# Batch 0 of a beacon-attention and maxout-FFN kernel: a new order of turns, score groups, quad loads and weight requests

## The chip, the cores and the metric

The kernel runs on one core of a Trainium2 chip. A core has five engines that work side by side: TensorE (PE in the profile; its weight loads are listed apart as PEld), VectorE (DVE), ScalarE (ACT), GpSimd (POOL) and SyncE (SP), which here only issues DMAs. Each engine runs its own instructions in order, and semaphores tie the engines together. The metric is the device time of one execution in microseconds; the median of several runs counts.

## What is computed

Attention with a causal mask, in which every query also sees 16 beacon keys without a mask, and behind it a feed-forward layer that takes the elementwise maximum of three projections. There are 8 batches of 8 heads, 576 tokens and a head size of 64; the model size is 512 and the inner size 768.

```python
scores = scale * np.matmul(q, k_all.transpose(0, 1, 3, 2))   # k_all, v_all: 16 beacons, then 576 tokens
scores = np.where(causal, -1000000000.0, scores)             # beacons are never masked
a = np.exp(scores - scores.max(-1, keepdims=True))
a /= a.sum(-1, keepdims=True) + 1e-09
attn = np.matmul(a, v_all)                                   # then x = attn as (tokens, 512)
h = np.maximum(np.maximum(x @ w1, x @ w2), x @ w3)
out = h @ w_out
```

## The kernel before

**Tiling.** Two heads make a pair (`p`, 4 pairs a batch, 32 in all), two pairs make a quad. Q and K of a pair are needed with the head dimension on partitions ("turned"). They are held in `qkT`, a ring of 4 pairs: first 576 columns of Q, then 16 beacon columns and 576 columns of K. For batches 0 to 3 PE turns them by transposes into PSUM, and DVE or ACT copies them out; for the later batches a DMA does it through DRAM.

**Steps of attention.** For a pair the scores are computed as K by Q in four groups (`emit_scores(p, gi)`): PE writes a two-bank tile `sc` of PSUM (two such tiles exist), and ACT takes the exponential of it into `at_sb` (line 469). `emit_masks` zeroes the causal part, on DVE with a table `tri` (L486) or on POOL with an affine select (L488). When both pairs of a quad are ready, `emit_pv(quad, hf)` multiplies by ones (for the sums) and by V, for one half `hf` of the queries (L532), into the two `pv` banks or, where it is asked for (`apart`), into two `fps` banks. `invert_sums` takes 1/sum as exp(-ln) on ACT (L552, L554), and `multiply` writes the result into `xT` on DVE (L564).

**FFN.** `emit_ffn` takes the next unit of a list: first units of the first matmul with weights 1 and 2 for half token blocks (L611), then units of the third weight (L592), then units of the second matmul (L628). Each unit is followed by a copy or a maximum on DVE. A unit is allowed once its part of `xT` is written.

**Order.** All runs under a schedule that is written out by hand. `start()` loads and turns the first pairs; then the list `first_steps` takes the 16 score groups of batch 0, each followed by the functions written beside it: `T` turns a half of a pair, `M` masks, `P` is attention times V, `V` casts a piece of the first V tile on POOL, `F` is an FFN unit, `CW` and `TW` cast and turn a quad of batch 1. From batch 1 on a loop takes two score groups, masks, PV and FFN units in turn, and calls what `plan` holds for the step. `next_load` takes the next load from a list; loads of q, k and v go through SP's DMA queue into a ring of 8 tiles `st`. The weights and the four-head quads of batch 0 are cast on the way and are requested by POOL (L309, L228). A gate is a one-column memset of the `st` tile by an engine: the DMA has to wait for it, and so can't start before that engine has come to that place of its queue.

**PSUM.** Two tiles `sc` of two banks, two `pv` banks, two `fps` banks. `keep_busy` issues matmuls on constants whose result nobody reads; it takes a bank for itself.

Of the kernel before, what the change touches and what calls it, by code (L numbers as in the profile page):

```python
# [16 lines left out]
def kernel(  # L17
# [13 lines left out]
    nc = tc.nc  # L31

    B, H, S, D = q.shape
    Nb = beacon_k.shape[2]
    NK = S + Nb
    scale = 1.0 / float(D) ** 0.5
    d_model, d_ff = moe_w1.shape
# [26 lines left out]
    n_quad = 2  # L64
    PPB = H // 2
# [4 lines left out]
    B_PE = 4  # L70
# [36 lines left out]
    def head(g, j):  # L107
        return 4 * g + j
# [29 lines left out]
    bT = const.tile([128, PPB, NB_PE], BF16, name="bT")  # L138
    bk32_0 = const.tile([Nb, H, D], FP32, name="bk32_0")
    bk16_0 = const.tile([Nb, H, D], BF16, name="bk16_0")  # L140
    bk32_1 = const.tile([NB_PE - Nb, H, D], FP32, name="bk32_1")
    bk16_1 = const.tile([NB_PE - Nb, H, D], BF16, name="bk16_1")
# [3 lines left out]
    busy = const.tile([128, 320], BF16, name="busy")  # L146
    nc.vector.memset(busy, 1.0)
    ident = const.tile([128, 128], BF16, name="ident")
# [4 lines left out]
    NT = 4  # L153
    qk_all = const.tile([128, NT, S + NKP], BF16, name="qkT")
    qkTs = [qk_all[:, i] for i in range(NT)]
    qTs = [z[:, 0:S] for z in qkTs]
    kTs = [z[:, S : S + NKP] for z in qkTs]
# [6 lines left out]
    def pv_bank(i, shape, dtype):  # L164
        return pv_psum.tile(shape, dtype, name=f"pv{i}")

    by_dve = nc.vector.tensor_copy
    by_act = nc.scalar.copy
    by_pool = nc.gpsimd.tensor_copy
# [8 lines left out]
    def new_stage(key):  # L178
        stage[key] = st_pool.tile([128, STW], FP32, name="st")
        return stage[key]  # L180

    def load_wide(quad, i, gate=None):
        b, g = divmod(quad, n_quad)
        st = new_stage(("wide", quad, i))

        if gate:
            gate.memset(st[:, 0:1], 0.0)
        src = (q, k)[i][b, head(g, 0) : head(g, 0) + 4]
        nc.sync.dma_start(
            out=st[:, 0 : 2 * WR * D].rearrange("p (x c) -> p x c", x=2),  # L190
            in_=src.rearrange("(x y) (p r) d -> (y p) x (r d)", y=2, r=WR),
        )
# [125 lines left out]
    def load_beacons(b0, b1, dst, queue=None):  # L318
        for b in range(b0, b1):
            (queue or nc.sync).dma_start(  # L320
                out=dst[Nb * (b - b0) : Nb * (b - b0 + 1)],
                in_=beacon_k[b].rearrange("h n d -> n h d"),
            )
# [60 lines left out]
        if r1 == WR:  # L384
            stage.pop(("wide16", quad, i))

    def turn_half(p, h, pv, q_copy=None):
        for i in range(2):
            src = stage.pop(("half16", p, h, i))
            if pv:  # L390
                bank = pv_bank(i, [128, 1024], BF16)
            else:
                bank = ffn_psum.tile([128, 1024], BF16, name="fps")
            ps = bank[:, 0:HALF]
            for r in range(HR):
                for e in range(2):
                    nc.tensor.transpose(
                        ps[64 * e : 64 * e + 64, r * QP : (r + 1) * QP],
                        src[:, e, r],
                        ident[0:QP, 0:QP],  # L400
                        tile_position=(0, 64 * e),
                    )
            x0 = i * Nb + HALF * h
            dst = (qTs, kTs)[i][p % NT][:, x0 : x0 + HALF]
            (q_copy if i == 0 and q_copy else by_dve)(
                dst.rearrange("d (p r) -> d p r", r=HR), ps.rearrange("d (r p) -> d p r", r=HR)
            )

    def place_beacons(p, copy):
        b, pi = divmod(p, PPB)  # L410
        copy(kTs[p % NT][:, 0:Nb], bT[:, pi, Nb * b : Nb * (b + 1)])

    def turn_quad(quad, i):
        for n, copy in enumerate((by_dve, by_act)):
# [10 lines left out]
    def keep_busy(n, cols=320, ffn=False):  # L425
        ps = ffn_psum.tile([128, 512], FP32, name="fps") if ffn else pv_bank(1, [128, 512], FP32)
        for _ in range(n):
            nc.tensor.matmul(
                ps[:, 0:cols], busy[:, 0:128], busy[:, 0:cols], start=True, stop=True
            )  # L430
# [267 lines left out]
    def at_step(p, g, *fns):  # L698
        plan.setdefault((p, g), []).extend(fns)

    def L(fn, *a):
        return lambda: fn(*a)

    def load_v_pieces(b):
        return [L(load_v, b, 0), L(load_v, b, 1)]

    def load_qk(b):
        if b < B_PE:
            return [L(load_wide, n_quad * b + g, i) for g in range(n_quad) for i in range(2)]
        return [L(load_pair, p) for p in range(b * PPB, (b + 1) * PPB)]  # L710

    loads = [L(load_v, 0, 0, nc.gpsimd), L(load_v, 0, 1), L(load_beacons, 1, B_PE, bk32_1)]
    loads += load_qk(1)[2:] + load_v_pieces(1)
    for b in range(2, B):
        if b == B_PE - 1:
# [3 lines left out]
    def next_load(n=1):  # L719
        for _ in range(n):  # L720
            if loads:
                loads.pop(0)()

    def C(fn, *a):
        def run():
            fn(*a)
            next_load()

        return run

    def start():
        keep_busy(12)
        load_half(0, 0, nc.sync)
        load_half(0, 1, nc.scalar)
        load_half(1, 0, nc.sync)
        load_beacons(0, 1, bk32_0, nc.scalar)
        load_half(1, 1, nc.scalar)
        make_identity(nc, ident)
        nc.gpsimd.memset(tri, 1.0)
        nc.gpsimd.affine_select(  # L740
            out=tri,
            in_=tri,
            compare_op=ALU.is_ge,
            fill=0.0,
            base=0,
            pattern=[[1, 128]],
            channel_multiplier=-1,
        )
        load_quad(1, 0)
        next_load(1)  # L750
        load_quad(0, 1)
        load_quad(1, 1)
        next_load(2)
        load_wide(n_quad, 0)
        cast_half(0, 0, by_dve)
        cast_half(0, 1, by_act)
        by_dve(bk16_0, bk32_0)
        turn_half(0, 0, False, by_act)
        keep_busy(4)
        turn_beacons(0, 1, bk16_0)  # L760
        for p in range(1, PPB):
            place_beacons(p, by_act)
        cast_half(1, 0, by_dve)
        cast_half(1, 1, by_dve)
        keep_busy(2)
        turn_half(1, 0, True)

    pv_at = {}

# [5 lines left out]

    def T(p, h, pv, q_copy=None, idle=0):
        def run():
            turn_half(p, h, pv, q_copy)

            if idle:  # L780
                keep_busy(idle, 128, pv)

        return run

    def M(p, gi, dve=False):
        return L(emit_masks, p, gi, dve)

    def P(quad, hf, apart=False, first=0, last=len(passes)):
        return L(emit_pv, quad, hf, first, last, apart)

    def V(t):
        return L(cast_first_v, t)

    def G(i):
        return L(load_wide, n_quad, i, nc.vector)

    def F(n):
        return lambda: [emit_ffn(END) for _ in range(n)]

    def CW(quad, i):  # L800
        return L(cast_wide, quad, i, by_pool)

    def TW(quad, i, n, act=False):
        return L(turn_wide, quad, i, n, by_act if act else by_dve, False)

    def cast_p():
        for g in range(n_quad):
# [5 lines left out]


    first_steps = [
        ((0, 0), []),
        ((1, 0), [T(2, 0, False), T(3, 0, True, by_act)]),
        ((2, 0), [L(keep_busy, 6, 128, True), V(0)]),
        ((3, 0), [T(0, 1, False, None, 6), M(0, 0, True), V(1), V(2), L(load_w, 0, 0, d_ff), L(load_w, 1, 0, d_ff)]),
        ((0, 1), [T(1, 1, True, None, 4), M(1, 0, True), M(0, 1)]),  # L820
        ((0, 2), [T(2, 1, False), M(0, 2), V(3), V(4)]),
        ((0, 3), [P(0, 0, False, 0, 2), M(2, 0, True), M(0, 3, True)]),
        ((1, 1), [T(3, 1, False), M(3, 0, True), M(1, 1)]),
        ((1, 2), [P(0, 0, False, 2, 4), invert_sums, M(1, 2)]),
        ((1, 3), [multiply, P(1, 0, True, 0, 2), M(1, 3, True)]),
        ((2, 1), [P(1, 0, True, 2, 4), invert_sums, M(2, 1), L(load_wide, n_quad, 1, nc.vector), CW(2, 0)]),
        ((2, 2), [P(0, 1, False, 0, 2), multiply, M(2, 2, True)]),
        ((2, 3), [P(0, 1, False, 2, 4), invert_sums, M(2, 3), cast_p]),
        ((3, 1), [F(1), M(3, 1, True), multiply]),
        ((3, 2), [F(1), L(turn_beacons, 1, B_PE, bk16_1), L(next_load, 6), M(3, 2)]),  # L830
        ((3, 3), [F(1), TW(2, 0, 0), M(3, 3), CW(2, 1), F(1), TW(2, 0, 1, True), P(1, 1), invert_sums, F(1), TW(2, 1, 0), 
                  TW(2, 1, 1, True), L(place_quad_beacons, 2, by_act), multiply]),
    ]
    at_step(4, 1, L(load_w, 2, 0, d_ff))
    at_step(4, 0, C(cast_wide, 3, 0, by_act))
    at_step(4, 1, C(cast_wide, 3, 1, by_act))
    at_step(5, 0, C(cast_v, 1, 0, by_pool))
    at_step(5, 1, C(cast_v, 1, 1, by_pool))
    at_step(6, 0, L(load_w_out))
    for quad in range(4, B_PE * n_quad):  # L840
        at_step(2 * quad - 3, 1, C(cast_wide, quad, 0, by_pool))
        at_step(2 * quad - 2, 1, C(cast_wide, quad, 1, by_pool))
    for b in range(2, B):
        p = b * PPB
# [6 lines left out]
    for b in range(B_PE, B):  # L851
        p = b * PPB
# [117 lines left out]
```

## Time and profile before

| What | us |
|---|---|
| median of 9 runs | 301.62 |
| lowest, highest of them | 300.63, 304.44 |
| the profiled execution | 300.94 |
| its span, first to last instruction | 299.2 |
| first scores of batch 0 | 6.98 |
| first scores of batch 1 | 35.84 |

In the profile a row of the timeline gives start and length in us, engine, line, operation, what is written and read, how many instructions are merged in the row, and in brackets how long the engine was idle before it and what ended the idle time. A row of a stretch gives its bounds and length, then for PE, weight loads, DVE, ACT and POOL the busy time (instructions), then the granted PE clock, the mean busy share of the 16 DMA engines (above 1 when packets overlap) and GB/s. The row of slices cuts the span into 40 parts of 7.5 us. Some of the largest groups of instructions are:

| Engine, line, what | count | mean ns |
|---|---|---|
| ACT L469 exponentials of a score group | 128 | 862 |
| PE L592 FFN matmuls into fps | 488 | 357 |
| DVE L602 maximum, 128x512 | 72 | 687 |
| POOL L237 cast of half a quad (q or k), 128x1152 | 10 | 1142 |
| ACT L237 the same | 2 | 1163 |
| POOL L299 cast of a piece of the first V, 128x512 | 4 | 614 |

### The profile page before, as it was taken

The page shows a single profiled execution, that of the slowest core. Times are in us where ns is not written, and L with a number is a line of the kernel's source. Part 1 is how long each engine was busy: PE and PEld are TensorE (multiplying, and loading weights), DVE is VectorE, ACT ScalarE, POOL GpSimd, SP SyncE. Part 2 cuts the span into 40 slices and gives each one's busy share as a digit, 9 for nine tenths or more (in the row PEclk, how much of TensorE's full clock was granted, in tenths as well). Part 3 has the DMA queues.
Part 4 walks back from the last instruction along what each step waited for, and adds up shares of the span by engine and source line. Part 5 has one row for each costly group of instructions (what it writes and reads, how often), then busy time and mean ns, then how long its engine had stood idle before and what let it go on. Part 6 is the DMA issues. An engine that isn't in the chain of part 4 may idle for free.

```text
span 299.2 us, 8583 instructions
## 1 busy us (share of the span) xinstructions
PE 285.9 (96%) x3556; PEld 153.4 (51%) x3556; DVE 173.2 (58%) x339; ACT 149.4 (50%) x235; POOL 120.1 (40%) x241
## 2 busy tenths in 40 slices
PE   7879898999999999999999999999999999999995
PEld 4546664554544545454545777544454544444442
DVE  4765456545767466636563757365746575274373
ACT  3866497785655465536463646364635431400300
POOL 7274068374446464546455544554233210000000
PEclk9978999999999999999999999999999999999999
DMA  8999999996939999999999999897212001103003
GB/s 144 214 205 298 205 348 216 210 334 165 226 87 200 211 263 218 189 191 303 226 211 186 280 238 191 198 256 130 56 54 90 2 0 72 70 2 121 21 2 140
DMA packets 83590, 50.66 MB, mean 169 GB/s; under 512 B 64224, under 2 KB 75232, under 8 KB 83552
## 3 DMA queue, kind: packets, MB, share of 16 engines
q1 hardware_dynamic: 78944, 45.76, 66.9%
q0 software_dynamic: 4048, 4.03, 8.3%
q8 instruction: 28, 0.46, 0.7%
q10 hardware_dynamic: 560, 0.33, 0.5%
q14 instruction: 10, 0.08, 0.1%
HBM read 35.13 MB, written 14.22 MB: 165 GB/s over the span
## 4 chain that ended last, share of the span: by engine, by line
PE 84%; DMA 6%; DVE 4%; ACT 2%; POOL 1%; issue 1%; SPq 1%; POOLq 0%; DVEq 0%
PE fps L592 32%; PE pv L532 13%; PE sc L592 12%; PE fps L628 11%; PE sc L460 8%; PE sc L628 4%; DMA st<-in_v_dram 3%; DMA w_sb<-in_moe_w_dram 3%; PE fps L611 2%; PE pv L373 1%; ACT at_sb L469 1%; DVE y L636 1%; PE fps L532 1%; DVE xT L564 1%; DVE at_sb L486 1%
## 5 line engine op out<-in xcount | busy, mean ns | idle before, releaser
L469 ACT ACTIVATE at_sb<-sc 128x928 bf16<-128x928 f32 (+5 forms) x128 | 104.1, 862 | 86.7 <-PE sc L460 84.8
L592 PE MATMUL fps<-xT,w_sb 128*128 128x512 bf16 (+1 forms) x488 | 110.3, 357 | 1.5 <-DMA w_sb<-in_moe_w_dram 1.0
L488 POOL TENSOR_SCALAR_AFFINE_SELECT at_sb<-at_sb 128x256 bf16<-128x256 bf16 (+2 forms) x148 | 53.9, 382 | 112.4 <-ACT at_sb L469 111.1
L592 PEld LDWEIGHTS <-w_sb 128*128 128x128 bf16 x672 | 61.5, 98 | 66.2 <-issue 12.0
L602 DVE TENSOR_TENSOR hT<-hT,fps 128x512 bf16<-128x512 bf16 x72 | 49.4, 687 | 34.7 <-PE fps L592 34.7
L592 PE MATMUL sc<-xT,w_sb 128*128 128x512 bf16 (+1 forms) x184 | 42.1, 356 | 0.0
L460 PE MATMUL sc<-qkT 64*128 64x288 bf16 (+5 forms) x400 | 36.3, 280 | 3.4 <-ACT at_sb L469 1.2
L628 PE MATMUL fps<-w_out_sb,hT 128*128 128x512 bf16 x150 | 36.0, 379 | 0.0
L636 DVE COPY y<-fps 128x512 f32<-128x512 f32 x25 | 17.3, 692 | 27.5 <-PE fps L628 24.7
L628 PEld LDWEIGHTS <-hT 128*128 128x128 bf16 x210 | 19.8, 98 | 24.1 <-DVE hT L602 1.9
L602 DVE TENSOR_TENSOR hT<-hT,sc 128x512 bf16<-128x512 bf16 x30 | 20.6, 687 | 16.4 <-PE sc L592 16.2
L532 PE MATMUL pv<-at_sb,v_sb 128*32 128x288 bf16 (+5 forms) x1376 | 29.7, 233 | 0.4 <-POOL v_sb L299 0.4
L600 DVE CAST hT<-fps 128x512 bf16<-128x512 f32 x31 | 21.4, 692 | 12.8 <-PE fps L592 12.8
L460 PEld LDWEIGHTS <-qkT 64*128 64x128 bf16 x400 | 14.5, 94 | 27.4 <-issue 21.4
L564 DVE TENSOR_TENSOR xT<-pv,recip 128x288 bf16<-128x288 f32 (+2 forms) x93 | 27.2, 348 | 2.2 <-ACT recip L554 2.2
L532 PEld LDWEIGHTS <-v_sb 128*32 128x32 bf16 (+1 forms) x1408 | 25.2, 98 | 3.4 <-issue 1.2
L248 POOL CAST p<-st 96x768 bf16<-96x768 f32 x32 | 25.5, 823 | 0.0
L287 POOL CAST v_sb<-st 128x1536 bf16<-128x1536 f32 (+2 forms) x21 | 18.4, 894 | 0.0
L532 PE MATMUL pv<-at_sb,ones 128*32 128x288 bf16 (+4 forms) x500 | 17.5, 261 | 0.0
L552 ACT ACTIVATE lnd<-pv 128x288 f32<-128x288 f32 x31 | 12.9, 417 | 6.1 <-PE pv L532 6.0
L532 PEld LDWEIGHTS <-ones 128*32 128x32 bf16 (+2 forms) x512 | 11.2, 97 | 8.6 <-issue 6.5
L600 ACT CAST hT<-sc 128x512 bf16<-128x512 f32 x6 | 3.5, 586 | 23.7 <-PE sc L592 23.7
(72 smaller groups left out, 177.4 us busy)
## 6 DMA issues: line engine op xcount, KB each, us to landing
out_dram<-y SPq DMA_DIRECT2D x35, 256.0 KB, 2.6
st<-in_v_dram SPq DMA_DIRECT2D x24, 256.0 KB, 5.3
st<-in_q_dram SPq DMA_DIRECT2D x16, 288.0 KB, 5.2
st<-in_k_dram SPq DMA_DIRECT2D x16, 288.0 KB, 5.7
st<-in_q_dram SPq DMA_DIRECT2D x6, 576.0 KB, 6.4
st<-in_k_dram SPq DMA_DIRECT2D x6, 576.0 KB, 7.8
w_sb<-in_moe_w_dram POOLq DMA_DIRECT2D x6, 384.0 KB, 8.5
q_dram<-p SPq DMA_DIRECT2D x16, 144.0 KB, 2.5
```

What stands on the lines that cost most here:

```text
L248: cast(part.rearrange("p r h d -> p h r d"), st[0:QP, i * NQ2 : (i + 1) * NQ2].rearrange("p (h r d) -> p h r d", h=2, r=QR),)
L287: cast(v_sb[0:n, t:t1].rearrange("p t h d -> p (t h d)"), st[0:n, (t - t_lo) * H * D : (t1 - t_lo) * H * D],)
L460: nc.tensor.matmul(ps[:, e, off : off + q1 - q0], kT[hs, 128 * t : 128 * t + 128], qT[hs, q0:q1], start=True, stop=True, tile_position=(64 ...
L469: nc.scalar.activation(out=both_heads(p, gi), in_=ps[:, :, 0 : g_width(p, gi)], func=AF.Exp, scale=scale)
L488: nc.gpsimd.affine_select(out=view, in_=view, compare_op=ALU.is_ge, fill=0.0, base=x0, pattern=[[0, 2], [1, hi - lo]], channel_multiplier=-1,)
L532: nc.tensor.matmul(ps[bank][32 * j : 32 * j + 32, lo + q0 - qa : lo + qb - qa], lhsT, at_view(pair_of(quad, j)[0], t, pair_of(quad, j)[1], ...
L564: nc.vector.tensor_mul(xT[:, 2 * g + part - 1, c0 + ca : c0 + cb], ps[bank][:, lo : lo + cb - ca], recip[:, ca:cb],)
L592: nc.tensor.matmul(ps[:, o0 : o0 + n], w_in[i][:, ct, 128 * ft : 128 * (ft + 1)], xT[:, ct, x0 : x0 + n], start=(ct == 0), stop=(ct == n_c ...
L600: (by_act if alone[0] else by_dve)(h, ps)
L602: nc.vector.tensor_max(h, h, ps)
L628: nc.tensor.matmul(ps, hT[:, ft, 128 * tt : 128 * (tt + 1)], w_out_sb[:, ft, :], start=(ft == 0), stop=(ft == n_ft - 1),)
L636: nc.vector.tensor_copy(y, ps)
```

## The change

- **Fillers.** `turn_half` gets `idle`: so many transposes of a constant, written into unused columns of the bank that the turn writes next. `T` passes its `idle` on; `keep_busy` is no longer called behind a turn, and the call after scores (2,0) is gone. Fillers stand at (1,0) and (3,0), 4 each.
- **Turns and score groups.** T(2,0) stands behind scores (0,0), ahead of (1,0). T(3,1) moves up to (0,3). P(0,0) moves behind (1,2) and (1,3), P(1,0) behind (2,1) and (2,2), P(0,1) behind (2,3) and (3,1). Masks of (2,2), (3,1), (3,2), (3,3) are all on DVE. Some q copies change between ACT and DVE.
- **Beacons.** Three copies on ACT become one for pairs 1 to 3.
- **Loads.** The second piece of V of batch 0 is issued in step (1,0), its first tile on ACT's queue, its second on SP's. The load of q of quad 2 leaves `start()`; it stands in step (2,2), gated by DVE; k of quad 2 follows it and has no gate of its own. `next_load` takes 5 at (3,2) instead of 6.
- **Weights.** The first is requested by POOL between V(1) and V(2), the second after V(4), the third in step (2,3) behind the cast of q of quad 2 (before: in step (4,1)), `w_out` in step (5,0) (before: (6,0)).
- **Casts and turns.** The casts of quad 3 go from ACT to POOL. Q of quad 2 is turned in the `pv` banks ahead of P(1,1).

```diff
-    def turn_half(p, h, pv, q_copy=None):
+    def fill(ps, n):
+
+        for i in range(n):
+            x0 = 512 + 128 * (i % 4)
+            nc.tensor.transpose(ps[:, x0 : x0 + 128], busy[:, 0:128], ident)
+
+    def turn_half(p, h, pv, q_copy=None, idle=0):
...
+            if i == 0:
+                fill(bank, idle)
...
-    loads = [L(load_v, 0, 0, nc.gpsimd), L(load_v, 0, 1), L(load_beacons, 1, B_PE, bk32_1)]
+    loads = [L(load_v, 0, 0, nc.gpsimd), L(load_v, 0, 1, None, (nc.scalar, nc.sync)), L(load_beacons, 1, B_PE, bk32_1)]
...
-        next_load(2)
-        load_wide(n_quad, 0)
...
-        for p in range(1, PPB):
-            place_beacons(p, by_act)
+        by_act(qk_all[:, 1:PPB, S : S + Nb], bT[:, 1:PPB, 0:Nb])
...
-        turn_half(1, 0, True)
+        turn_half(1, 0, True, by_act)
...
-        ((0, 0), []),
-        ((1, 0), [T(2, 0, False), T(3, 0, True, by_act)]),
-        ((2, 0), [L(keep_busy, 6, 128, True), V(0)]),
-        ((3, 0), [T(0, 1, False, None, 6), M(0, 0, True), V(1), V(2), L(load_w, 0, 0, d_ff), L(load_w, 1, 0, d_ff)]),
-        ((0, 1), [T(1, 1, True, None, 4), M(1, 0, True), M(0, 1)]),
-        ((0, 2), [T(2, 1, False), M(0, 2), V(3), V(4)]),
-        ((0, 3), [P(0, 0, False, 0, 2), M(2, 0, True), M(0, 3, True)]),
-        ((1, 1), [T(3, 1, False), M(3, 0, True), M(1, 1)]),
-        ((1, 2), [P(0, 0, False, 2, 4), invert_sums, M(1, 2)]),
-        ((1, 3), [multiply, P(1, 0, True, 0, 2), M(1, 3, True)]),
-        ((2, 1), [P(1, 0, True, 2, 4), invert_sums, M(2, 1), L(load_wide, n_quad, 1, nc.vector), CW(2, 0)]),
-        ((2, 2), [P(0, 1, False, 0, 2), multiply, M(2, 2, True)]),
-        ((2, 3), [P(0, 1, False, 2, 4), invert_sums, M(2, 3), cast_p]),
-        ((3, 1), [F(1), M(3, 1, True), multiply]),
-        ((3, 2), [F(1), L(turn_beacons, 1, B_PE, bk16_1), L(next_load, 6), M(3, 2)]),
-        ((3, 3), [F(1), TW(2, 0, 0), M(3, 3), CW(2, 1), F(1), TW(2, 0, 1, True), P(1, 1), invert_sums, F(1), TW(2, 1, 0), 
-                  TW(2, 1, 1, True), L(place_quad_beacons, 2, by_act), multiply]),
+        ((0, 0), [T(2, 0, False)]),
+        ((1, 0), [T(3, 0, True, None, 4), L(next_load, 2), V(0)]),
+        ((2, 0), []),
+        ((3, 0), [T(0, 1, False, None, 4), M(0, 0, True), V(1), L(load_w, 0, 0, d_ff), V(2)]),
+        ((0, 1), [T(1, 1, True), M(1, 0, True), M(0, 1)]),
+        ((0, 2), [T(2, 1, False), M(2, 0, True), M(0, 2), V(3), V(4), L(load_w, 1, 0, d_ff)]),
+        ((0, 3), [T(3, 1, False), M(3, 0, True), M(0, 3, True)]),
+        ((1, 1), [M(1, 1)]),
+        ((1, 2), [P(0, 0, False, 0, 2), M(1, 2)]),
+        ((1, 3), [P(0, 0, False, 2, 4), invert_sums, M(1, 3, True)]),
+        ((2, 1), [P(1, 0, True, 0, 2), multiply, M(2, 1), cast_p]),
+        ((2, 2), [P(1, 0, True, 2, 4), invert_sums, M(2, 2, True), G(0), L(load_wide, n_quad, 1)]),
+        ((2, 3), [P(0, 1, False, 0, 2), multiply, M(2, 3), CW(2, 0), L(load_w, 2, 0, d_ff)]),
+        ((3, 1), [P(0, 1, False, 2, 4), invert_sums, F(1), M(3, 1, True)]),
+        ((3, 2), [F(1), multiply, L(turn_beacons, 1, B_PE, bk16_1), L(next_load, 5), M(3, 2, True)]),
+        ((3, 3), [F(1), M(3, 3, True), CW(2, 1), L(turn_quad, 2, 0), F(1), TW(2, 1, 0), P(1, 1), invert_sums, TW(2, 1, 1, True),
+                  L(place_quad_beacons, 2, by_act), F(1), multiply]),
     ]
-    at_step(4, 1, L(load_w, 2, 0, d_ff))
-    at_step(4, 0, C(cast_wide, 3, 0, by_act))
-    at_step(4, 1, C(cast_wide, 3, 1, by_act))
+    at_step(4, 0, C(cast_wide, 3, 0, by_pool))
+    at_step(4, 1, C(cast_wide, 3, 1, by_pool))
...
-    at_step(6, 0, L(load_w_out))
+    at_step(5, 0, L(load_w_out))
```

More of the change, by code (lines that the diff above doesn't have):

```diff
@@ L407, in turn_half @@
             )
-    def place_beacons(p, copy):
-        b, pi = divmod(p, PPB)
-        copy(kTs[p % NT][:, 0:Nb], bT[:, pi, Nb * b : Nb * (b + 1)])
     def turn_quad(quad, i):
@@ L777, in run @@
         def run():
-            turn_half(p, h, pv, q_copy)
-            if idle:
-                keep_busy(idle, 128, pv)
+            turn_half(p, h, pv, q_copy, idle)
         return run
```

## The prediction

> **What bounds the kernel now.** I read the time row, then the 40 slices, then stretches of some 5 us, then the chain of waits and the timeline where TensorE (PE) is not full. The page first:
>
> ```profile
> span 299.2 us, 8583 instructions
> PE 285.9 (96%) x3556; PEld 153.4 (51%) x3556; DVE 173.2 (58%) x339; ACT 149.4 (50%) x235; POOL 120.1 (40%) x241
> ...
> PEclk9978999999999999999999999999999999999999
> DMA  8999999996939999999999999897212001103003
> ```
>
> PE is busy 96% of the span, and from about 54 us on it is never short of work until the tail. The change touches only work before that. The stretches say where those 50 us lose time (PE busy first, then weight loads, DVE, ACT, POOL, granted clock, DMA share, GB/s):
>
> ```profile
> 10.00:15.00 5.00, 4.43 (x86) 2.58 (x83) 4.07 (x15) 4.13 (x5) 1.55 (x3) 1.00 1.33 217
> 15.00:20.00 5.00, 3.53 (x66) 1.79 (x66) 4.34 (x10) 2.96 (x5) 4.95 (x11) 0.83 0.87 183
> 20.00:25.00 5.00, 5.00 (x106) 3.08 (x106) 1.32 (x7) 3.06 (x5) 1.65 (x2) 0.50 1.08 243
> 36.00:42.00 6.00, 5.69 (x60) 4.05 (x57) 2.86 (x5) 5.74 (x7) 2.87 (x7) 1.00 1.02 316
> ```
>
> From 15 to 25 us PE starves or runs at half clock (0.50) while ACT, which has all the exponentials, works only 3 of each 5 us. From 36 to 42 ACT is full (5.74 of 6). The timeline names the waits:
>
> ```profile
> 14.67 0.61 POOL L299 CAST v_sb<-st 128x512 bf16<-128x512 f32 x1 [0.54 <-DMA st<-in_v_dram]
> 15.90 1.67 ACT L469 ACTIVATE at_sb<-sc 128x992 bf16<-128x992 f32 x2 [1.05 <-PE sc L460]
> 20.85 1.00 ACT L469 ACTIVATE at_sb<-sc 128x992 bf16<-128x992 f32 x1 [1.96 <-PE sc L460]
> 35.84 0.54 PE L460 MATMUL sc<-qkT 64*128 64x288 bf16 x8 [0.89 <-ACT qkT L420]
> 37.82 1.15 ACT L237 CAST p<-st 128x1152 bf16<-128x1152 f32 x1
> 50.33 0.61 PE L592 MATMUL fps<-xT,w_sb 128*128 128x512 bf16 x2 [1.03 <-DMA w_sb<-in_moe_w_dram]
> ```
>
> So: P(0,0), the first product with V, stands in PE's queue ahead of the scores of (1,1) and waits for a V cast that ends at 15.3; ACT sits idle behind it. A second idle of 1.96 us follows, when P(1,0) waits for a mask. At 50.33 PE waits 1.03 us for the third weight, requested only at 40.86. My marker is the first score group of batch 1, at 35.84 now.
>
> **Part by part.** Profiled run: 300.94 us for a span of 299.2. I walked the new order through block by block: each starts when its engine's queue, its inputs and its buffer are free, and takes its row's duration. The same walk of the old order puts the marker at 35.5, 0.3 from the trace.
>
> *Start to exp(0,1).* T(2,0) is put ahead of scores (1,0). Its k half needs a quad transfer whose completion events end at 7.87, so scores (1,0) run at 8.06 to 8.49 instead of 7.70 to 8.10; their exponential starts at 8.53 instead of 8.39: +0.14. Beacons: three ACT copies (0.41 in all) become one, about 0.21 by the nearest row (128x32, 0.21). The q copy of pair 1 goes to ACT (0.41), that of pair 3 leaves it (0.41). Both lie in ACT's 0.73 us idle ahead of exp(0,0) or balance: 0. Fillers: 16 small ones in three groups (0.51, 0.51, 0.40 us as busy rows) become 8 in two; they stand before transposes that wait for DMA or copies anyway: 0, the clock apart (below).
>
> *The V tile moved to ACT's DMA queue.* ACT now issues it after exp(1,0). The nearest rows are ACT's own issues at the start, 0.41 to 0.47 us. Other end: SP's issues of the same tiles, 2.46, 2.35 and 3.22 us, where SP's queue was backed up. The Trainium skill, "DMA: Bandwidth & Descriptors", section "Issuing engines are not separate DMA queues", speaks against this edit: other issuers only save sequencer time, since all share the same 16 DMA engines. By that rule there is no gain in bandwidth at all, and the DMA share of 1.33 at 10 to 15 us agrees; SP is nobody's bottleneck there, so the edit buys little and its price falls on the engine that paces. By ACT's row that price is 0.45, by SP's up to 3.2. I take 0.45, for ACT's queue is empty. exp(2,0) then starts at 9.95 instead of 9.79. exp(0,1) waits for the same quad landing (10.83) as before and starts at 12.10 against 12.06: 0.
>
> *exp(0,1) to exp(3,3).* Before, ACT needs 12.06 to 28.96: 16.9 us. Its work there is 4 x (1.00+0.76+0.65) of exponentials = 9.64, three Ln/reciprocal pairs at 0.86 = 2.6, one 0.32 copy: 12.6; so 4.3 us are idle. After: scores (0,3), (1,1), (1,2) stand ahead of P(0,0), which starts at about 15.1 and stalls 0.5 us for the V cast (POOL now issues the first weight, 2 x 0.55, between V1 and V2: V2 at 15.85) while ACT still has exp(1,1) and (1,2) to 16.9. The 1.05 and 1.96 idles go. What is left: 0.21 for quad k of (2,1) at 13.56, 0.40 for turn copies on DVE, 0.2 for the first FFN unit (its weight lands about 22.5), 0.3 for the beacon turn, about 1.2 in all. Last exp ends 12.1+12.6+1.2 = about 25.9: 3.0 us sooner.
>
> *Quads of batch 1.* Here some is given back. wide(2,0) was requested at 15.68; now it is behind a memset on DVE that is queued behind mask (2,2), which waits for exp(2,2): about 20.5 to 21. On SP everything of batch 1 is queued behind it. In the profile the pair took 15.7 to 23.4 and 20.3 to 29.14, each some 5.5 us once moving, beside the weights. So I put wide(2,0) at 26 and wide(2,1) at 28.5. POOL casts them (1.14 each, with the issue of w2, 1.1, between): 27.2, then 29.7. PE, free at 26.0, waits 1.3 us for the first and 0.7 for the second. Then, in order: turn 0.45, P(1,1) 1.7, Ln and reciprocal 0.9, turn copy 0.74, beacons 0.21, so scores (4,0) at 29.7 + 4.3 with gaps = 34.0; with V and quads half a us later through the extra queue, **34.3** against 35.84: **-1.5**. Its bounds: landing of wide(2,1) at 27 gives 33.3; one more us of landing costs one us.
>
> *Casts of quad 3 from ACT to POOL.* ACT is full from 36.27 to 45.8; 2 x 1.16 us leave. PE's own idle in 36 to 46 is 0.95 us (0.31+0.64), so that is the ceiling; POOL takes 2.28 and loses the issue of w2 (1.09) and sits idle 6.9 us before this stage. Floor 0. Near full, since ACT was the cause: **-0.6**.
>
> *w2 about 13 us sooner, w_out one step sooner.* The 1.03 us wait at 50.33 goes: **-1.0**. Behind it: DMA is saturated from 19 to 60 us and w2 needs 3.8 us of it (0.79 MB written at the 209 GB/s that this queue reached at 22 to 24 us). The V tiles of batch 1, ahead of which it now goes, landed by 37.19 for a cast at 43.48: 6.3 us of slack, less 3.8, less the some 2 us by which the need comes sooner: 0.5. Cost 0, with up to 1.5 if DMA lags. One prefetch fewer (5 for 6): in the waits from 60 us on POOL's casts wait for no load, so 0.
>
> Sum: -1.5 - 0.6 - 1.0 = **-3.1**: 297.8 for a run like the profiled one. That run lies 0.7 under the median of the nine (301.62), so the median becomes **298.5**.
>
> **The clock.** PE's clock is 0.50 from 18.28 to 25.11 by the trace's clock record. In the walk a full clock moves the old marker by only 0.2 us, for ACT paces, so I count nothing for it. The Trainium skill, "TensorE: Matmul & The Clock Gate", section "HAM oscillation — how this bites in real kernels", says to avoid PE-idle gaps over about 3.4 us. The row disagrees: before 18.28 no gap was longer than about 1.1 us, yet the clock fell. By the rule the new order, with half the fillers, has nothing to fear, cost 0. By the row, the stretch 11.5 to 14.9, where I make PE only some 60% busy, may drop it: half speed for 6.8 us, +0.9 at the marker; or a drop at 28 to 35, where PE does wait for the quads, +2.
>
> **Rivals.**
> - *The gated quad loads take the stall's place (slower side).* For it: the loads start 5 us later, DMA showed only 0.87 at 15 to 20 us and will be emptier there, and w1 and w2 run beside them; wide(2,1) took 8.8 us from request. Against: the weights are further on by then. Marker = landing + 5.3 plus the half us above; the 1.6 of the later stages is kept, so it decides from a landing at about 31.6. At 33.5: 303.5 for the median.
> - *ACT stands in its DMA issue* (SP's 3.2 us and more, as if its own queue were backed up too). Exponentials then start 3 to 3.5 late and the gate with them; marker about 36.3; 36.3-35.84-1.6 = -1.1: 300.5. Against: ACT's queue is separate and empty in the rows.
> - *Clock falls again in a worse place*: +0.9 to +2: 299.4 to 300.5.
> - *It doesn't do what it says*: exponentials no earlier because the turn copies on DVE (0.41 each, twelve of them, with the masks at 0.58 between) pace instead; only -1.6 is left: 300.0.
>
> **Chances.** Forecast 0.50; gate 0.22 (over half of it slower by more than 0.5%); ACT issue 0.11; clock 0.10; DVE 0.07. A measurement of this kernel can tell about 0.5% (1.5 us) from no change. Under 300.1: all of the forecast, most of clock and DVE: 0.62. Over 303.1: 0.18. Between: 0.20. Range: 296.3 (marker at 33, both later gains full) to 303.3 (gate).
>
> **What would show it.** Right: ACT's idles of 1.05 and 1.96 gone and the last exp of batch 0 near 26; first scores of batch 1 at 33 to 35; no w_sb wait near 47 to 50; ACT no longer full in the 10 us after the marker. Wrong: an ACT issue row above 1 us near 9.5; POOL's cast of quad 2 waiting for st beyond 29; scores of batch 1 after 36; POOL or PE waiting for V of batch 1.

## The result, and the profile after

The changed kernel takes 299.95 us (median of 18 runs, 298.48 to 302.30); the kernel before takes 301.62. The ratio is 0.9933 with a 95% interval of 0.991 to 0.9956: some 2.0 us, or 0.7%, faster (1.7 us by the two medians). 298.5 was forecast, with a range of 296.3 to 303.3.

The profiled execution after took 301.02 us, with a mean TensorE clock of 0.975, and is one of the longer runs: of the 19 with a clock record twelve show 0.982 or 0.983, with a median of 299.67 us, and seven 0.975 to 0.977, with 300.74. The two profiled executions, before and after, are equally long (spans of 299.2 and 299.3 us). So the rows serve to see where time is lost and won, and the ratio to say how much in all.

The page of the profile after, the same rows as before:

```profile
span 299.3 us, 8565 instructions
PE 287.5 (96%) x3548; PEld 153.5 (51%) x3548; DVE 172.7 (58%) x341; ACT 147.3 (49%) x231; POOL 121.4 (41%) x241
...
PEclk9958799999999999999999999999999999999999
DMA  8999989977937999999999999898422001103003
```

Slices 3 to 5 (15 to 37 us) carry a low clock; the one slice ahead of the tail in which the DMA engines are mostly idle, at 82 to 90 us, is still there. The stretches, with the same columns as before:

```profile
10.00:15.00 5.00, 3.68 (x70) 2.32 (x72) 3.85 (x15) 3.75 (x5) 2.10 (x4) 0.99 1.33 216
15.00:20.00 5.00, 4.97 (x82) 2.03 (x82) 2.91 (x11) 3.98 (x7) 4.03 (x9) 0.50 1.02 178
20.00:25.00 5.00, 5.00 (x110) 3.13 (x108) 1.14 (x5) 2.89 (x5) 1.84 (x6) 0.50 0.98 181
...
30.00:36.00 6.00, 4.84 (x99) 3.57 (x99) 3.06 (x4) 0.84 (x2) 2.79 (x4) 0.72 1.21 238
36.00:42.00 6.00, 5.42 (x60) 3.80 (x54) 2.96 (x7) 4.58 (x8) 2.96 (x7) 1.00 0.82 172
```

From 15 to 20 us TensorE no longer starves (4.97 for 3.53; in part only because each product takes longer at half clock: 82 instructions, for 66) and ACT has a full us more work (3.98 for 2.96): the new order does feed ACT there. But the clock is now at 0.50 for all ten us instead of 6.8, and a second fall shows at 30 to 36 (0.72). In the 10 us after the first scores of batch 1 ACT is no longer full (busy 7.70 us, for 9.53 before). The timeline names the waits:

```profile
15.55 1.67 ACT L473 ACTIVATE at_sb<-sc 128x992 bf16<-128x992 f32 x2 [0.52 <-PE sc L464]
24.18 1.00 ACT L473 ACTIVATE at_sb<-sc 128x992 bf16<-128x992 f32 x1 [1.49 <-PE sc L464]
27.89 0.66 ACT L473 ACTIVATE at_sb<-sc 128x576 bf16<-128x576 f32 x1
30.68 0.68 PE L373 MATMUL pv<-ident,p 128*128 128x128 bf16 x9 [1.93 <-POOL p L237]
37.54 0.55 PE L464 MATMUL sc<-qkT 64*128 64x288 bf16 x8 [0.28 <-ACT qkT L424]
46.91 0.55 PE L464 MATMUL sc<-qkT 64*128 64x288 bf16 x8 [0.23 <-DVE qkT L380]
49.60 1.04 PE L596 MATMUL fps<-xT,w_sb 128*128 128x512 bf16 x4
```

The idle of 1.05 us ahead of the exponentials near 15.6 has halved. The last exponential of batch 0 starts at 27.89 and ends near 28.55 (before 28.96). TensorE then stands 1.93 us for the cast of quad 2, and the marker (first scores of batch 1) comes at 37.54, **1.7 us later** than before. From there 1.7 us are won back: the units of the third weight (from 49.60) run without the wait of 1.03 us, and the 9.37 us from the marker to the next TensorE wait for a copy (46.91) were 10.17 before, from 35.84 to this row:

```profile
46.01 0.55 PE L460 MATMUL sc<-qkT 64*128 64x288 bf16 x8 [0.23 <-DVE qkT L380]
```

The chain of waits (start, length, what) shows why the turn was late:

```profile
21.59 0.07 DVE st L187
21.66 0.02 issue
21.68 7.67 DMA st<-in_q_dram
...
29.48 1.14 POOL p L237
30.62 1.02 POOL w_sb L309 x2
31.64 1.16 POOL p L237
32.80 0.05 issue
32.85 0.71 PE fps L373 x5
```

The gate's memset runs at 21.59, the request leaves at once, and 7.67 us later the first half of quad 2 is there; POOL casts it, issues the third weight, and casts the other half. All of this is on the chain.

### The profile page after: what moved, and what is told of

Read it like the earlier page. It is cut to its first block, busy times and chain, and to the rows that moved or that the text cites. A ratio compares the mean times of both kernels' runs of the same rounds, so it can differ in the third digit from the quotient of the medians.

```text
span 299.3 us, 8565 instructions
## 1 busy us (share of the span) xinstructions
PE 287.5 (96%) x3548; PEld 153.5 (51%) x3548; DVE 172.7 (58%) x341; ACT 147.3 (49%) x231; POOL 121.4 (41%) x241
## 4 chain that ended last, share of the span: by engine, by line
PE 85%; DMA 5%; DVE 3%; POOL 3%; ACT 2%; issue 1%; POOLq 0%; DVEq 0%
PE fps L596 32%; PE pv L536 13%; PE sc L596 12%; PE fps L632 11%; PE sc L464 9%; PE sc L632 4%; DMA quad<-in_k_dram 3%; DMA st<-in_q_dram 3%; PE pv L373 1%; PE fps L615 1%; POOL quad L228 1%; ACT at_sb L473 1%; DVE qkT L380 1%; POOL p L237 1%; DVE y L640 1%
## 5 line engine op out<-in xcount | busy, mean ns | idle before, releaser
L492 POOL TENSOR_SCALAR_AFFINE_SELECT at_sb<-at_sb 128x256 bf16<-128x256 bf16 (+2 forms) x146 | 53.1, 383 | 105.4 <-ACT at_sb L473 104.6
L536 PE MATMUL pv<-at_sb,v_sb 128*32 128x288 bf16 (+5 forms) x1376 | 30.7, 236 | 0.0
L536 PE MATMUL pv<-at_sb,ones 128*32 128x288 bf16 (+4 forms) x500 | 18.2, 268 | 0.0
L237 POOL CAST p<-st 128x1152 bf16<-128x1152 f32 x12 | 13.7, 1143 | 6.4 <-DMA st<-in_q_dram 6.4
```

Source lines behind the costliest of these rows:

```text
L492: nc.gpsimd.affine_select(out=view, in_=view, compare_op=ALU.is_ge, fill=0.0, base=x0, pattern=[[0, 2], [1, hi - lo]], channel_multiplier=-1,)
L536: nc.tensor.matmul(ps[bank][32 * j : 32 * j + 32, lo + q0 - qa : lo + qb - qa], lhsT, at_view(pair_of(quad, j)[0], t, pair_of(quad, j)[1], ...
```

## The experiments

Two theories stood at first. **A**: the late landing of quad 2 sets the marker, because its gated request stands behind the second weight in the DMA engines; the clock costs time only where TensorE paces. **B**: the clock at half speed sets it. All runs were timed in five rounds beside the kernel before, whose median was 301.88, 301.36 and 301.78 us in the three groups of four.

**Quad 2's first half early.** Its load is requested in step (1,0) without a gate; the gate goes to the second half.

```diff
-        ((1, 0), [T(3, 0, True, None, 4), L(next_load, 2), V(0)]),
+        ((1, 0), [T(3, 0, True, None, 4), L(next_load, 2), L(load_wide, n_quad, 0), V(0)]),
-        ((2, 2), [..., G(0), L(load_wide, n_quad, 1)]),
+        ((2, 2), [..., G(1)]),
```

> The changed kernel with one edit: the load of q of quad 2 is requested in step (1,0) again, without a gate, and the gate by DVE in step (2,2) stands ahead of k of quad 2. Theory A (the late quads set the first scores of batch 1; they came late because the gated request at 21.7 stood behind the second weight in the DMA engines): q of quad 2 lands at about 23.5 instead of 29.35, PE's wait of 1.93 us for its cast goes, scores (4,0) at about 35 instead of 37.5, time 1.5 to 2.5 us below the changed kernel, ratio to the kernel before about 0.986 to 0.989. Theory B (the half clock from 14.9 to 25.1 sets it, PE being full there): the wait goes but PE comes no sooner, so at most 0.5 us, ratio 0.992.

298.28 us, ratio 0.9876 with a 95% interval of [0.9836, 0.9915]. The first half landed at 19.26 by the trace, the second at 28.72. A stretch, and the rows of the turn and the marker:

```profile
15.00:20.00 5.00, 5.00 (x84) 2.17 (x83) 3.54 (x13) 3.74 (x6) 4.09 (x8) 0.50 1.14 230
```

```profile
28.52 0.66 PE L373 MATMUL pv<-ident,p 128*128 128x128 bf16 x9
34.02 0.55 PE L464 MATMUL sc<-qkT 64*128 64x288 bf16 x8 [0.27 <-ACT qkT L424]
```

The clock falls much as in the changed kernel, yet the turn waits for no quad, and the marker comes 3.5 us sooner than its 37.54: 2.2 of them stand at the start of the turn (28.52 for 30.68), the rest behind it, where the clock does not fall a second time. Nor is it chance in the clock: at a mean of 0.983 the four runs of this kernel have a median of 298.14 us, the ten of the changed one 299.78. So the late quad sets the marker, as A says; why it was late is another question (below).

**More fillers.** Fillers from some 10 to 17 us, 10 and 6 ahead of both halves of T(2,1) and T(3,1), and a group of six at two more places; quads as changed.

```diff
-            if i == 0:
+            if i == 0 or idle > 4:
                 fill(bank, idle)
-        ((2, 0), []),
+        ((2, 0), [L(keep_busy, 6, 128, True)]),
-        ((3, 0), [T(0, 1, False, None, 4), M(0, 0, True), V(1), L(load_w, 0, 0, d_ff), V(2)]),
+        ((3, 0), [T(0, 1, False, None, 4), L(keep_busy, 6, 128), M(0, 0, True), V(1), L(load_w, 0, 0, d_ff), V(2)]),
...
-        ((0, 2), [T(2, 1, False), M(2, 0, True), M(0, 2), V(3), V(4), L(load_w, 1, 0, d_ff)]),
-        ((0, 3), [T(3, 1, False), M(3, 0, True), M(0, 3, True)]),
+        ((0, 2), [T(2, 1, False, None, 10), M(2, 0, True), M(0, 2), V(3), V(4), L(load_w, 1, 0, d_ff)]),
+        ((0, 3), [T(3, 1, False, None, 6), M(3, 0, True), M(0, 3, True)]),
```

> The changed kernel with more fillers from 8 to 15 us: a bank's fillers also ahead of the k half where more than 4 are asked for, 10 at T(2,1), 6 at T(3,1), and six matmuls on constants behind scores (2,0) and behind T(0,1). Both theories: the clock holds at 1.00 past 14.9. Theory A: PE then reaches the turn of quad 2 by about 26.5 and waits 3 to 4 us there, so the first scores of batch 1 stay near 37 and the time moves by 0 to -0.7 us, ratio 0.991 to 0.994. Theory B: last exponential of batch 0 near 26 instead of 28.5, time 2 us lower, ratio 0.987. If the fillers do not hold the clock, it is the same as the changed kernel or 0.3 us worse.

299.77 us, ratio 0.9926 [0.9896, 0.9956]: no better than the changed kernel.

```profile
15.00:20.00 5.00, 4.96 (x113) 3.04 (x110) 3.94 (x12) 3.27 (x6) 3.80 (x8) 1.00 1.08 183
20.00:25.00 5.00, 4.79 (x131) 3.23 (x124) 2.22 (x9) 4.92 (x9) 2.49 (x7) 1.00 0.95 168
```

```profile
26.46 0.66 ACT L473 ACTIVATE at_sb<-sc 128x576 bf16<-128x576 f32 x1
30.02 0.68 PE L373 MATMUL pv<-ident,p 128*128 128x128 bf16 x9 [2.70 <-POOL p L237]
36.85 0.54 PE L464 MATMUL sc<-qkT 64*128 64x288 bf16 x8 [0.28 <-ACT qkT L424]
```

With a full clock ACT works 4.92 of 5 us at 20 to 25 and starts the last exponential of batch 0 at 26.46, 1.4 us sooner than the changed kernel; then TensorE waits 2.70 us for the same quad, and behind that wait the clock falls after all (from 31.24 to 34.65 by its record). So B by itself does not explain the time. It is not nothing either: the three of the 11 runs with a mean clock of 1.000 have a median of 298.73 us, the other eight 299.99.

**Both**, the first half early and the fillers.

> Both edits, the early load of q of quad 2 and the added fillers. Theory A: either edit frees what the other leaves, so the sum is more than the two alone: scores (4,0) at 33.5 to 34.5, time 3 to 3.5 us below the changed kernel, ratio about 0.982 to 0.984. Theory B: as the fillers alone, ratio 0.987.

299.29 us, ratio 0.9912 [0.9881, 0.9943]: above the early load alone by the medians (the intervals overlap), and outside of what either theory expected. In the profiled run TensorE arrived early and waited for the second half, still gated, whose load took 9.03 us from request to landing (22.02 to 31.05; 6.79 without the fillers), and the clock fell behind that wait:

```profile
30.00:36.00 6.00, 3.63 (x88) 3.14 (x89) 1.41 (x2) 1.23 (x3) 1.14 (x1) 0.80 1.12 255
```

```profile
32.37 0.45 PE L373 MATMUL fps<-ident,p 128*128 128x128 bf16 x5 [2.51 <-POOL p L237]
```

Of its 16 runs, eight with a mean clock of 0.994 have a median of 300.45 us; the other eight, at 0.998 to 1.000, have 297.70. So here some 2.7 us go with the fall; only one run was traced, where the fall comes with the wait for the quad, and the two are not told apart by this.

**Both halves early, without and with the fillers.** The second half is requested behind the first, ungated; the gate moves on to quad 3's first load. The second run adds the fillers of above.

```diff
-        ((1, 0), [T(3, 0, True, None, 4), L(next_load, 2), V(0)]),
+        ((1, 0), [T(3, 0, True, None, 4), L(next_load, 2), L(load_wide, n_quad, 0), L(load_wide, n_quad, 1), V(0)]),
-        ((2, 2), [..., G(0), L(load_wide, n_quad, 1)]),
+        ((2, 2), [...]),
-    loads += load_qk(1)[2:] + load_v_pieces(1)
+    loads += [L(load_wide, n_quad + 1, 0, nc.vector), L(load_wide, n_quad + 1, 1)] + load_v_pieces(1)
```

> The changed kernel with both loads of quad 2 requested in step (1,0), ahead of the third V tile, with no gate; the gate goes to quad 3's first load. If late landings set the first scores of batch 1, the second half of quad 2 now lands by 24 us, TensorE waits for no quad cast ahead of its turn, and the first scores of batch 1 come at 33 to 34 us whatever the clock does: ratio 0.982 to 0.988. If the clock at half speed sets it, the clock still falls for 10 us and the time stays at 0.993. A side cost: V tiles 2 to 4 of batch 0 and the first weight come later by up to 2 us, which would show as POOL or TensorE waiting for V near 17 to 22 us.

> The same with the added fillers at 8 to 15 us. If the fall of the clock at 32 us in the two earlier runs with these fillers came from TensorE waiting over 2 us for a quad cast, it does not fall now: clock 0.998 or above in all runs, first scores of batch 1 at 32.5 to 33.5 us, ratio 0.980 to 0.985. If the fillers only move the fall to a later place, the clock stays at 0.983 to 0.994 and the ratio at 0.987 to 0.992.

Without: 298.69 us, 0.9897 [0.9861, 0.9934], marker at 34.20 and no wait for a quad. The second half landed at 26.14, later than I said, the ratio is above what I expected, and there was a side cost: TensorE waits 0.87 us, until 25.75, for the first weight, whose second part landed at 25.71 (21.26 in the changed kernel). With the fillers: **297.08 us, 0.986 [0.9819, 0.99]**, the best of the study and faster than both kernels, if short of the 0.980 to 0.985 that I expected; the clock was 0.997 or above in all six runs. Its stretches and marker:

```profile
10.00:15.00 5.00, 4.91 (x88) 3.40 (x84) 3.71 (x13) 3.57 (x5) 1.92 (x4) 1.00 1.36 216
15.00:20.00 5.00, 4.96 (x112) 2.98 (x110) 3.23 (x12) 3.71 (x7) 3.41 (x8) 1.00 1.14 253
20.00:25.00 5.00, 3.51 (x108) 2.27 (x104) 1.94 (x7) 3.71 (x7) 4.48 (x10) 1.00 1.09 227
```

```profile
28.04 0.66 ACT L473 ACTIVATE at_sb<-sc 128x576 bf16<-128x576 f32 x1
33.96 0.54 PE L464 MATMUL sc<-qkT 64*128 64x288 bf16 x8 [0.27 <-ACT qkT L424]
```

By the medians the fillers give 1.6 us more once the quads are in time (the intervals overlap). But the last exponential of batch 0 starts at 28.04 and the marker comes at 33.96, each only 0.24 us sooner than without them, while the profiled runs lie 1.1 us apart in span (295.6, 296.7). The rest arises at 44 us. Without the fillers POOL's cast of V of batch 1 waits 1.02 us for its load and starts at 42.03, and a mask behind it in POOL's queue holds TensorE:

```profile
44.77 0.56 PE L536 MATMUL pv<-at_sb,ones 128*32 128x176 bf16 x7 [0.36 <-POOL at_sb L492]
```

With them the cast waits 0.18 us and starts at 40.96, and no mask holds TensorE there. So most of this difference is a V load that lands sooner or later; that the fillers bring it about is not shown.

**The third weight alone, on the kernel before.**

```diff
-        ((2, 3), [P(0, 1, False, 2, 4), invert_sums, M(2, 3), cast_p]),
+        ((2, 3), [P(0, 1, False, 2, 4), invert_sums, M(2, 3), cast_p, L(load_w, 2, 0, d_ff)]),
-    at_step(4, 1, L(load_w, 2, 0, d_ff))
```

> The kernel before with one edit: the third weight is requested by POOL at the end of step (2,3) instead of step (4,1). If the term of the prediction for it is right, PE's wait of 1.03 us for the weight near 50 goes and nothing takes its place: 1.0 us less, ratio 0.9967. Rival: the weight's 3.8 us of DMA delay the quads and V of batch 1 and the same is lost there: ratio 0.999 to 1.003.

300.50 us, ratio 0.9951 [0.9925, 0.9977], some -1.5 us where -1.0 was forecast (the interval holds both); the wait of 1.03 us is gone. The marker, the end of the stage and the first unit of the third weight:

```profile
36.42 0.54 PE L460 MATMUL sc<-qkT 64*128 64x288 bf16 x8 [0.89 <-ACT qkT L420]
46.60 0.55 PE L460 MATMUL sc<-qkT 64*128 64x288 bf16 x8 [0.23 <-DVE qkT L380]
49.29 1.04 PE L592 MATMUL fps<-xT,w_sb 128*128 128x512 bf16 x3
```

**The casts of quad 3 alone, and with the third weight, on the kernel before.**

```diff
-    at_step(4, 0, C(cast_wide, 3, 0, by_act))
-    at_step(4, 1, C(cast_wide, 3, 1, by_act))
+    at_step(4, 0, C(cast_wide, 3, 0, by_pool))
+    at_step(4, 1, C(cast_wide, 3, 1, by_pool))
```

> The kernel before, with one edit: the two casts of quad 3 in steps (4,0) and (4,1) go from ACT to POOL. The prediction priced this edit at -0.6 us (ratio 0.998), ACT being full between 36 and 42 us. A rival says that TensorE's own gaps there come from something else, so that nothing is gained: ratio 1.000, ACT's busy time at 36 to 42 us falls from 5.7 of 6 to 4.6 or less, and TensorE's stays at 5.7.

> The kernel before with the third weight requested at the end of step (2,3) and the casts of quad 3 by POOL, both together. If the two terms of the prediction add up, this is 0.6 us better than the early weight alone (ratio 0.9951): 0.993. The casts alone gave nothing, although the scores of pair 7's first group came 0.8 us sooner against the marker, because TensorE met the wait for the third weight at 50.1 us all the same; with that wait gone the gain should come out. If the casts are worth nothing in any company, the ratio stays at 0.995.

Alone: 301.48 us, 0.9999 [0.9974, 1.0025]: no gain, though the interval would hold the forecast -0.6 us as well. Three rows of that run, the marker, the wait at the end of the stage and the next wait for the weight:

```profile
36.59 0.54 PE L460 MATMUL sc<-qkT 64*128 64x288 bf16 x8 [0.89 <-ACT qkT L420]
...
45.97 0.55 PE L460 MATMUL sc<-qkT 64*128 64x288 bf16 x8 [0.23 <-DVE qkT L380]
50.13 0.60 PE L592 MATMUL fps<-xT,w_sb 128*128 128x512 bf16 x2 [0.87 <-DMA w_sb<-in_moe_w_dram]
```

The stage shrank from 10.17 us to 9.38, by 0.8, but the weight, requested on the same step as before, stops TensorE at 50.13 all the same (before 50.33). Together: 299.71 us, 0.9929 [0.9906, 0.9952], 0.7 us better than the weight alone as I expected, and in the profiles the stage is 9.37 us (the rows below), for 10.18 with the weight alone. The two intervals overlap, so that the 0.7 rests on the rows more than on the ratio.

```profile
36.46 0.55 PE L460 MATMUL sc<-qkT 64*128 64x288 bf16 x8 [0.89 <-ACT qkT L420]
45.83 0.55 PE L460 MATMUL sc<-qkT 64*128 64x288 bf16 x8 [0.23 <-DVE qkT L380]
```

**The new order without its weights and casts**: third weight at (4,1), `w_out` at (6,0) and quad 3's casts on ACT, as before; with the quads as changed, then with both halves of quad 2 early.

```diff
-        ((2, 3), [P(0, 1, False, 0, 2), multiply, M(2, 3), CW(2, 0), L(load_w, 2, 0, d_ff)]),
+        ((2, 3), [P(0, 1, False, 0, 2), multiply, M(2, 3), CW(2, 0)]),
-    at_step(4, 0, C(cast_wide, 3, 0, by_pool))
-    at_step(4, 1, C(cast_wide, 3, 1, by_pool))
+    at_step(4, 1, L(load_w, 2, 0, d_ff))
+    at_step(4, 0, C(cast_wide, 3, 0, by_act))
+    at_step(4, 1, C(cast_wide, 3, 1, by_act))
-    at_step(5, 0, L(load_w_out))
+    at_step(6, 0, L(load_w_out))
```

> The changed kernel with the third weight, the output weight and the casts of quad 3 put back to where they were: what is left is the new order in batch 0, the gated quad loads, the beacons, the V tile on ACT's queue and the fillers. The prediction priced that part at -1.5 us (ratio 0.995). If the late quads have eaten it, as the profile of the changed kernel says (first scores of batch 1 at 37.5 us instead of 35.8), it gives +0.5 to +1.7 us: ratio 1.002 to 1.006, with the first scores of batch 1 at 36.5 to 37.5 us.

> The changed kernel with quad 2 requested early and without a gate, and with the third weight, the output weight and the casts of quad 3 where they were before: the new order by itself, with its quads in time. The prediction's term for the order was -1.5 us: ratio 0.995, first scores of batch 1 at about 34.3 us, and the wait for the third weight back at 48 to 51 us, longer than the 1.03 us of before. If that wait swallows what the order wins, as it did with the casts, the ratio is 0.999 to 1.000 and the wait is 2 us or more.

As changed: 302.12 us, 1.0026 [0.9999, 1.0053], so nothing won and up to 0.5% lost. (The execution that was profiled was the longest of its 22, 305.02 us, so its rows are not used.) With the quads in time: 301.60 us, 0.9972 [0.9944, 1.0]: between both expectations. Here is the whole pattern in one run, the marker 1.7 us sooner than before and the weight's wait grown from 1.03 to 3.48 us:

```profile
34.12 0.55 PE L464 MATMUL sc<-qkT 64*128 64x288 bf16 x8 [0.26 <-ACT qkT L424]
...
50.85 0.60 PE L596 MATMUL fps<-xT,w_sb 128*128 128x512 bf16 x2 [3.48 <-DMA w_sb<-in_moe_w_dram]
```

The request stands in the same step as before and so came 1.7 us sooner too, but its load took longer and landed 0.5 us later. From the chains of this run and of the kernel before:

```profile
39.69 11.12 DMA w_sb<-in_moe_w_dram
41.41 8.88 DMA w_sb<-in_moe_w_dram
```

In this run the loads of batch 2's two quads were requested beside it (38.40 to 40.18 us), before some 4 us ahead of it (35.90 to 37.61); that this made it longer was not tested.

**The second weight one step sooner**, in the changed kernel and in the best one.

```diff
-        ((3, 0), [..., V(1), L(load_w, 0, 0, d_ff), V(2)]),
+        ((3, 0), [..., V(1), L(load_w, 0, 0, d_ff), V(2), L(load_w, 1, 0, d_ff)]),
-        ((0, 2), [..., V(3), V(4), L(load_w, 1, 0, d_ff)]),
+        ((0, 2), [..., V(3), V(4)]),
```

> The changed kernel, gate kept, with the second weight requested one step sooner, right behind the third V tile's cast (some 3 us sooner than 18.7 us). If the gated quad load of 21.7 us stood behind the second weight in the DMA engines, the weight is now through by some 23 us and the first half of quad 2 lands at 27 us or sooner instead of 29.35, the second at 28.5 instead of 30.85, first scores of batch 1 at 35.5 us, ratio 0.988 to 0.990. If the request takes its 7.7 us anyway, landing at 29 us and ratio 0.993. A cost on the other side: quads and V tiles of batch 0 landing later at 15 to 18 us.

> The early quads with the added fillers, and the second weight requested one step sooner as well. TensorE's 0.58 us wait for that weight at 25.5 us goes; ACT paces there, so the gain is small: ratio 0.984 to 0.986 (0.986 without it). If the weight's traffic delays quads and V tiles of batch 0 at 15 to 19 us, it is 0.988 or more.

In the changed kernel: 298.97 us, 0.9911 [0.9873, 0.9949]. The gated request left at 21.75 and landed at 27.83 (6.1 us, for 7.67), the second half at 29.34 (30.85):

```profile
29.16 0.68 PE L373 MATMUL pv<-ident,p 128*128 128x128 bf16 x9 [0.64 <-POOL p L237]
35.32 0.54 PE L464 MATMUL sc<-qkT 64*128 64x288 bf16 x8 [0.27 <-ACT qkT L424]
```

The landings and the marker came 1.5 and 2.2 us sooner, near what A expects. But this does not show the second weight to be the cause: in the run with more fillers, where that weight was requested as in the changed kernel, the same load took 6.48 us (22.21 to 28.69). Each figure is of one execution, and the intervals of the two kernels overlap. How much of the 7.67 us the second weight makes stays open.

In the best kernel the edit brought nothing (298.32 us, 0.9867 [0.9822, 0.9912]), and the expectation misread the wait: at 25 us TensorE waits for the first weight, not for the second. The second part of the first weight landed at 25.47 us without the edit and at 25.32 with it, and TensorE goes on right behind:

```profile
25.51 0.83 PE L615 MATMUL fps<-xT,w_sb 128*128 128x256 bf16 x6 [0.58 <-DMA w_sb<-in_moe_w_dram]
25.37 0.83 PE L615 MATMUL fps<-xT,w_sb 128*128 128x256 bf16 x6 [0.80 <-DMA w_sb<-in_moe_w_dram]
```

That part was requested at 14.77 and 14.63 us, behind both quad halves, and took 10.7 us each time; in the changed kernel, with no quad ahead of it, 6.57. So the edit moved a weight that TensorE did not wait for. A sooner request of the first weight was not tried.

## Why the prediction was right, and where it was not

The sign and the range held, and the sum of -3.1 us was 1.1 us too large by the ratio. Its terms did not hold alike, and that the number came so near is in part luck: the term for the order and the quads missed by 2.3 us, and the other terms together gave 1.2 us more than was written for them. Two of the prediction's own signs of being wrong came true: POOL's cast of quad 2 waited for its load until 29.35, and the first scores of batch 1 came after 36; of its signs of being right only the two behind the marker did, the weight's wait gone and ACT no longer full.

- **Order and quads, -1.5**: this failed. The same part by itself measured 1.0026 [0.9999, 1.0053], which is +0.8 us, and in the profile of the changed kernel the marker came 1.7 us later instead of 1.5 sooner. Three steps of it were mis-sized.
  - "wide(2,0) at 26 and wide(2,1) at 28.5": 29.35 and 30.85. The request left at 21.68, some 1 us later than said, and then "some 5.5 us once moving" was the wrong length, since a load that is held back by a gate must be counted from its request: 7.67 us here. The profile before had it: from its request at 15.68 to its landing at 23.40 the same load took 7.72.
  - "Last exp ends ... about 25.9: 3.0 us sooner": 28.55, 0.4 sooner. The wait of 1.05 at 15.90 shrank and that of 1.96 went, but others came. From the end of exp(0,1) on the profile after has seven waits of ACT for TensorE, 4.6 us in all, where 1.2 was counted; the kernel before has five there, with 4.8. A full clock cures about half of the miss, at the price of the fillers' own time: with them alone ACT ends at 27.1. The two errors cover each other in part: TensorE was expected at the quad at 26.0 and waiting 1.3, came at 28.75 and waited 1.93.
  - "I count nothing" for the clock: it fell where the row of before said it might (11.5 to 14.9: PE 3.68 of 5 us at 10 to 15, falling at 14.9), and again after the wait at 30 us. By this trace the row beat the rule of the Trainium skill that was set against it ("TensorE: Matmul & The Clock Gate", section "HAM oscillation — how this bites in real kernels"): no gap of TensorE was near 3.4 us. All 19 runs of the changed kernel have a mean clock of 0.983 or less, but only 31 of 133 of the kernel before. The cost named there, +0.9 and +2, fits the marker of the kernel with more fillers (0.7 sooner with the first fall gone) and the groups of runs with more and with fewer falls (1.1 us in the changed kernel, 2.7 with the early half and the fillers, the wait included). What the clock costs the changed kernel in all stays open.
- **What the order is worth with its quads in time**: the marker is at 33.8 to 34.2 in five kernels, close to the 34.3 of the prediction, although by another path: TensorE comes later than was said and waits for no quad. Without the gate on quad 2 the whole change gives 0.9897, or -3.1 us: the sum as it was written. The first rival, the gated loads that take the stall's place, is what happened, in a milder form (landing 30.85; it was to decide from 31.6).
- **Casts, -0.6**: the size was right (0.8 in the rows of the stage, 0.7 by ratios), but the term isn't free-standing: in the rows of the casts alone the wait for the third weight takes it. It was added to the sum as if it were.
- **Third weight, -1.0**: -1.5 alone. From "order alone" (1.0026) to the whole change (0.9933) it is 2.8 us with the casts and `w_out` (which was not run alone), while the weight and the casts on the kernel before give 2.1; the intervals do not tell these two apart. The 1.7 us won behind the marker match the 1.6 of the sum.
- **V tile on ACT's queue at 0.45**: its issue row is 0.40 us, beside an exponential; the rival of a backed-up queue fell.

Two sums of the working are off by little: 34.0 with half a us more is 34.5, not 34.3 (landing + 5.3 + 0.5 does give 34.3), and a marker at 33 with both later gains full gives about 296.8, not 296.3.

So the change is faster through its weights and casts; its new order, delayed by its own gate, paid nothing back on this kernel.

## What to carry to other kernels

A stage that is made earlier moves its needs forward: list the loads behind it with the times of their request and their landing. A request in the same step moves along, but its load need not land sooner, and the gain turns into a wait (1.03 to 3.48 us here). A gate on a load must be priced from the request to the landing, as the profile before has it for the same load, not from the rate of a load already moving. Before a request is moved, find by landing times which load the wait is for. Put two gains behind one wait in series, not in a sum: the second shows only when the wait is gone.

## What was not expected of the hardware

- The clock fell with TensorE busy 3.68 of 5 us and without a gap above 0.8 us from 10 us to the fall at 14.88, and stayed at 0.50 for 10.2 us although the profile then shows TensorE busy 4.97 and 5.00 of 5. With fillers that made it 4.91 of 5 it stayed at 1.00, and then kept 1.00 through a stretch of 3.51 of 5 us (20 to 25 us of the best kernel).
- By the clock records every stretch at half clock in the fourteen profiles lasts 3.41, 6.83 or 10.24 us, that is one, two or three times 3.41; why is not shown. By an estimate from this, 3.41 us at half clock in a span of 299 lower the mean clock by 0.0057, so that 0.994, 0.989, 0.983 and 0.977 stand for one to four times 3.41 us.
- In the 133 timed runs of the kernel before with a clock record, 11 with a mean clock of 1.000 have a median of 300.56 us, 47 at 0.992 to 0.999 have 301.07, 44 at 0.986 to 0.989 have 302.15 and the 31 at 0.983 or less 303.35: the same program meets a fall in some executions and none in others, and the time goes with it by up to 2.8 us. The walk of the old order had put a fall at 0.2. (This is a correlation; no run set the clock of the old order on purpose.)
- The 16 completion events of one load are spread: those of the gated half came from 26.38 to 29.35 us, those of the same load before from 21.87 to 23.40. Its consumer waits for the last, so 3 us of its 7.67 are this spread.
